# A windowed-attention and Mish feed-forward kernel: TensorE's instructions fixed in the program's order from chunk 2 on, an attention pair's values joined with the next pair's scores, and priorities for a step's functions

## The chip, the cores and the metric

The kernel runs on one core of one Trainium2 chip. The metric is the time in microseconds (us) of one execution on the device, from its start to its end. Three executions of the kernel before gave 993.93, 995.66 and 997.05 us, so the median is 995.66 us. A profiled execution is a fourth one; its own time is used where its trace is read.

A core has five engines that run side by side. TensorE (PE in the profile) multiplies matrices into PSUM; its weight loads are shown apart as PEld. VectorE (DVE), ScalarE (ACT) and GpSimd (POOL) do elementwise work. SyncE (SP) here only issues DMA transfers. The program gives each engine its own list of instructions; one that waits for another engine holds up those behind it on its list.

## The reference, cut to what matters

```python
def _attn_ref(q, k, v):                      # q, k, v: (8, 8, 576, 64)
    scores = scale * np.matmul(q, k.transpose(0, 1, 3, 2))
    rel = pos[:, None] - pos[None, :]
    mask = (rel >= 0) & (rel < 64)           # a window of 64 keys
    scores = np.where(mask, scores, -1e9)
    scores = scores - np.max(scores, axis=-1, keepdims=True)
    attn = np.exp(scores)
    attn = attn / (np.sum(attn, axis=-1, keepdims=True) + 1e-09)
    return np.matmul(attn, v)

def _moe_ref(x, w_in, w_out):                # x: (4608, 512), d_ff = 2048
    h = x @ w_in
    sp = np.where(h > 20.0, h, np.log1p(np.exp(np.minimum(h, 20.0))))
    g = h * np.tanh(sp)
    return g @ w_out
```

The output of the attention, with the heads laid side by side, is the `x` of the feed-forward part. All is float32.

## The kernel before, in words

**Chunks, steps and pairs.** The 4608 tokens are cut into 12 chunks of 384. The feed-forward part of a chunk is 16 *steps*, one for each 128 of the 2048 hidden columns. A step has a first product (`ffn_in`, 12 matmuls of 128x384 into one PSUM tile `h_ps`, line 195), a chain of functions, and a second product (`ffn_out`, 9 matmuls of 128x512 into the three sums `acc`, line 230). Twelve and nine, because every float32 factor is split into a high and a low part (`xh`, `xl`; `wi_h`, `wi_l`; `gh`, `gl`; `wo_h`, `wo_l`) and three of the four products are taken. The functions of a step run on DVE (line 202), ACT (203, 208, 209, 210), DVE (212) and POOL (216, 217; ACT line 214 in chunk 0). `h_ps` has two buffers, and line 212 is its last reader. The second product of a step is put into the program two steps behind its first one (`LAG = 2`).

The attention of a chunk is done in four *pairs* of heads. A pair has `scores` (24 small matmuls into two `s_ps`, line 128, then the masked minimum on DVE, line 138, six exponentials on ACT, line 141, and the normalisation on DVE, lines 149 to 151), `transpose`, and `values` (24 small matmuls into `o_ps`, line 184, then `xh` on ACT, line 186, and `xl` on DVE, line 187). For chunks 1 and 2 the transpose is six TensorE transposes (line 171) with a copy out of PSUM on ACT and one on DVE (line 172). For chunks 3 and up it is one DVE transpose of 32x32 blocks (line 160) and twelve DMA transfers from `tr` to `pT`, issued by SP (line 165).

**The weights** are loaded and split during chunk 0's steps (`load_w`): DVE lines 252 to 256 and 258, ACT lines 251 and 257, POOL lines 252 and 258.

**What sets the order.** The first 8 steps belong to chunk 0; then steps of chunks 0 and 1 alternate; from chunk 2 on one chunk follows the other. Each step has two *slots*. The attention of a chunk is a list of events with a slot each: scores at `begin + p*step`, transpose at `+0.6*step`, values at `+lag*step`. In the loop a step's `ffn_in` is traced, then the events due by slot 2n, then the `ffn_out` of two steps back, then the events due by slot 2n+1:

```python
    for n, (c, f) in enumerate(steps):
        ...
        pend.append((c, f, ffn_in(c, atts[c].x, f, c == NCHUNK - 1)))
        run(2 * n)
        if len(pend) > LAG:
            flush()
        run(2 * n + 1)
```

For chunks 3 and up the events begin with the first step of the chunk before and are 6 slots (3 steps) apart, values one spacing after the scores. So the values of pair p and the scores of pair p+1 are due in the same slot; the key puts the values first.

This trace order isn't the order on the engines. The kernel is built with `schedule_with_timeline_sim=True`: a planner goes through a simulated time and gives each engine the next instruction that is ready by then, and among ready ones the one that was traced first. What is ready depends on the planner's cost of each instruction and on free buffers (`h_ps` 2; the tag `at` for `s_ps`, `t_ps`, `o_ps` 3; `t` 4, shared by the functions and the splitting of weights; `pr` 2, shared by `pr` and `tr`). So a group of 12, 9 or 24 matmuls may come out in pieces with other work between them. The order that results is fixed in the program; the chip waits where an instruction isn't ready.

Of the kernel before, what the change touches and what calls it, by code (L numbers as in the profile page):

```python
# [2 lines left out]

# [15 lines left out]
BLK = 64  # L19
TINY = float(np.array(0x38000000, np.uint32).view(np.float32))  # L20
BIG = float(np.array(0x47EFFFFF, np.uint32).view(np.float32))
WP = 512


@with_exitstack
def tile_window_attn_mish_ffn(
# [60 lines left out]
    pTs = itertools.cycle(pTs)  # L87

    sums = itertools.cycle([f"acc{t}" for t in range(NTT)])
# [25 lines left out]
    def att_scores(c, p, tiles):  # L118
        q_t, k_t = tiles
        s_ps = [bank(c, p, "s_ps").rearrange("p (m k) -> p m k", k=P) for _ in range(2)]  # L120
        pr = ap_.tile([P, HM, P], F32, name="pr", bufs=2)
        mx = ap_.tile([P, HM], F32, name="mx", bufs=3)
        sm = ap_.tile([P, HM], F32, name="sm", bufs=3)
        for m in range(NM):
            for par, h in ((0, 0), (1, 1), (1, 0), (0, 1)):
                n = 2 * m + par
                rows = slice(h * BLK, (h + 1) * BLK)
                nc.tensor.matmul(s_ps[h][par * BLK:(par + 1) * BLK, m, :],  # L128
                                 q_t[rows, n * BLK:(n + 1) * BLK], k_t[rows, n * BLK:n * BLK + P],
                                 start=True, stop=True)  # L130
        for h in range(2):
            js = slice(h * NM, (h + 1) * NM)
            for m in range(NM):
                first = [(c * NB + 2 * m + par) % blocks_per_seq == 0 for par in range(2)]
                mk = firsts[first.index(True)] if any(first) else mask
                j = h * NM + m

                nc.vector.tensor_tensor_reduce(  # L138
                    out=pr[:, j, :], in0=s_ps[h][:, m, :], in1=mk,
                    op0=ALU.add, op1=ALU.min, scale=-0.125, scalar=3.0e38, accum_out=mx[:, j:j + 1])  # L140
                nc.scalar.activation(pr[:, j, :], pr[:, j, :], AF.Exp, bias=mx[:, j:j + 1], scale=-1.0,  # L141
                                     accum_out=sm[:, j:j + 1])
            if c == 0:

                nc.vector.tensor_scalar(sm[:, js], sm[:, js], 1e-9, None, ALU.add)
                nc.vector.reciprocal(sm[:, js], sm[:, js])
                nc.vector.tensor_tensor(pr[:, js, :], pr[:, js, :], sm[:, js].unsqueeze(2).to_broadcast([P, NM, P]), ALU.mult)
        if c > 0:
            nc.vector.tensor_scalar(sm, sm, 1e-9, None, ALU.add)
            nc.vector.reciprocal(sm, sm)  # L150
            nc.vector.tensor_tensor(pr, pr, sm.unsqueeze(2).to_broadcast([P, HM, P]), ALU.mult)
        return pr

    def att_transpose(c, p, pr):
        pT = next(pTs)
        if c > 2:


            tr = ap_.tile([P, P // 32, HM, 32], F32, name="tr", tag="pr", bufs=2)
            nc.vector.transpose(tr.rearrange("p k j i -> p j k i"),  # L160
                                pr.rearrange("p j (k i) -> p j k i", i=32))
            for r in range(0, P, 32):
                for k in range(0, P, 32):
                    if 0 <= k - r % BLK <= BLK:
                        nc.sync.dma_start(pT[k:k + 32, r // 32, :, :], tr[r:r + 32, k // 32, :, :])
            return pT
        for h in range(2):
            t_ps = (bank(c, p, "t_ps") if c else ps_h.tile([P, CH], F32, name="t_ps", tag="h_ps")
                    ).rearrange("p (m k) -> p m k", k=P)
            for m in range(NM):  # L170
# [4 lines left out]
        return pT  # L175

    def att_values(c, p, v_t, pT, x):
        xh, xl = x
        o_ps = bank(c, p, "o_ps")
        for n in range(NB):  # L180
            m, par = n // 2, n % 2
            for h in range(2):
                rows = slice(h * BLK, (h + 1) * BLK)
                nc.tensor.matmul(o_ps[rows, n * BLK:(n + 1) * BLK], v_t[:, n, rows],  # L184
                                 pT[:, 2 * par:2 * par + 2, h * NM + m, :], start=True, stop=True)
        nc.scalar.copy(xh[:, p, :], o_ps)
        nc.vector.tensor_tensor(xl[:, p, :], o_ps, xh[:, p, :].bitcast(F32), ALU.subtract)

    def ffn_in(c, x, f, alone=False):
        xh, xl = x  # L190
# [1 line left out]
        n = 0  # L192
        for cc in range(NC_):
            for w, xx in ((wi_h, xh), (wi_h, xl), (wi_l, xh)):
                nc.tensor.matmul(h_ps, w[:, f, cc, :], xx[:, cc, :], start=n == 0, stop=n == 3 * NC_ - 1)  # L195
# [6 lines left out]
        nc.vector.tensor_scalar(t, h_ps, 20.0, None, ALU.min)  # L202
        nc.scalar.activation(t, t, AF.Exp)  # L203
        if alone:

            h = ap_.tile([P, CH], F32, name="h", tag="pr", bufs=2)
            nc.scalar.copy(h, h_ps)
        nc.scalar.activation(t, t, AF.Square, bias=one_b)  # L208
        nc.scalar.activation(t, t, AF.Ln, bias=half_b, scale=0.5)  # L209
        nc.scalar.activation(t, t, AF.Exp, scale=-1.0)  # L210

        nc.vector.scalar_tensor_tensor(t, t, -1.0, h, ALU.add, ALU.mult)  # L212
        if c == 0:
            nc.scalar.copy(gh, t)  # L214
        else:
            nc.gpsimd.tensor_scalar(gh, t, 1.0, 0.0, ALU.mult, ALU.add)  # L216
        nc.gpsimd.tensor_tensor(gl, t, gh.bitcast(F32), ALU.subtract)  # L217
        return gh, gl

    half_b = const.tile([P, 1], F32, name="half_b")  # L220
# [4 lines left out]
    def ffn_out(acc, gg, f):  # L225
        gh, gl = gg
        for t in range(NTT):
            ts_ = slice(t * P, (t + 1) * P)
            for i, (a, w) in enumerate(((gh, wo_h), (gh, wo_l), (gl, wo_h))):
                nc.tensor.matmul(acc[t], a[:, ts_], w[:, f, :],  # L230
                                 start=f == 0 and i == 0, stop=f == NF - 1 and i == 2)

    def ffn_store(c, acc):
        for t in range(NTT):
            o = mp.tile([P, DO], F32, name="o", bufs=3, tag="st")
            if t % 2 == 0:
                nc.scalar.mul(o, acc[t], -1.0)
            else:
                nc.vector.tensor_scalar(o, acc[t], -1.0, None, ALU.mult)
            nc.sync.dma_start(out[c * CH + t * P:c * CH + (t + 1) * P, :], o)  # L240

    def load_w(src, wh, wl, first):
# [25 lines left out]
    class Att:  # L268
# [11 lines left out]
                getattr(a, what)[p] = {"qk": load_qk, "v": load_v}[what](a.c, p)  # L280

        def scores(self, p):
            self.pr[p] = att_scores(self.c, p, self.qk[p])
            self.load(p + 2, "qk")

        def transpose(self, p):
# [2 lines left out]
        def values(self, p):  # L289
            if self.x is None:  # L290
                self.x = tuple(xp.tile([P, NC_, CH], F32R, name=f"x{n}{self.c % 2}") for n in "hl")
            att_values(self.c, p, self.v[p], self.pT.pop(p), self.x)
            self.load(p + 2, "v")

        def plan(self, begin, step, lag=1):
# [65 lines left out]
    take_w(1)  # L361
    atts[1].plan(0, 2 * HEAD / (NPAIR + 1))
    atts[2].plan(third, (starts[2] - third) / (NPAIR + 1), 1.5)
    for c in range(3, NCHUNK):
        atts[c].plan(starts[c - 1], (2 * NF - 2) / (NPAIR + 1))
    events.sort(key=lambda e: e[:2])
    for n, (c, f) in enumerate(steps):
        if f == 0:

            while any(fn.__self__ is atts[c] for _, _, fn, _ in events):  # L370
                run(events[0][0])
        pend.append((c, f, ffn_in(c, atts[c].x, f, c == NCHUNK - 1)))
        run(2 * n)
        if len(pend) > LAG:
            flush()
        run(2 * n + 1)
        if c == 0:
            take_w(2)
    while pend:
        flush()  # L380


# [33 lines left out]
```

## Time and profile before

| | |
|---|---|
| median of three executions | 995.66 us (993.93 to 997.05) |
| the profiled execution | 995.3 us, of which 993.5 us from its first to its last instruction |
| mean granted TensorE clock | 0.972 |
| PE busy | 946.5 us (95%) |
| DVE, ACT, POOL busy | 491.8, 631.4, 328.8 us |
| chain that ended last | PE 87%, DVE 6%, DMA 2%, ACT 2% |

The chain of waits is followed back from the last instruction; its shares say which engine's work set the end. A matmul's duration in the trace is longer than the time to the next start, because matmuls overlap. So this document takes the cost of a group of matmuls from starts: from its first start to the first start of what follows.

In the rows of the timeline the columns are start and duration in us, engine, line, operation, `out<-in`, tile sizes, how many were merged into the row, and in brackets the idle time before it and what ended that. In the rows of waits they are who waited, for whom, the total in us, how many times, the longest. In the rows of windows they are the window, its length, busy time and instructions of each engine, the granted clock, the share of DMA and GB/s.

### The profile page before, as it was taken

Reading aid. Unit: us, or ns where it says so; the run is one execution under the profiler, and the core shown is the slowest. Engines: PE = TensorE matmul, PEld = TensorE weight load, DVE = VectorE, ACT = ScalarE, POOL = GpSimd, SP = SyncE. Lnnn points to the kernel's source line nnn. Section 1 sums busy time; section 2 is a strip of 40 time slices with the busy share of each in tenths; the row PEclk is TensorE's granted clock in tenths of the full one; section 3 lists DMA queues with packets and bytes.
Section 4 is the critical chain, followed back from the end, with each engine's and each line's share of the span. In section 5 each row is a group of like instructions: output and inputs, shape, how many; then the busy total and the mean of one; then the engine's idle time right before and its main releaser. Section 6 shows DMA issues by size and latency. Waiting matters only on the chain.

```text
span 993.5 us, 18088 instructions
## 1 busy us (share of the span) xinstructions
PE 946.5 (95%) x6408; PEld 821.4 (83%) x6408; DVE 491.8 (50%) x1352; ACT 631.4 (64%) x1525; POOL 328.8 (33%) x419
## 2 busy tenths in 40 slices
PE   4696699998999999999999999999999999999998
PEld 3585599886888888888888888888888888888996
DVE  6799874444444454444454453453443543543222
ACT  5667676664666666665665666666665665666664
POOL 2243463321333333323333323323333333333333
PEclk8787899997999999999999999999999999999999
DMA  7565420123221221331221221221231221310000
GB/s 240 188 194 161 143 85 1 49 68 111 66 69 54 89 69 42 88 83 42 88 83 43 89 81 45 86 83 46 84 80 47 85 74 43 97 39 13 32 1 32
DMA packets 82649, 77.34 MB, mean 78 GB/s; under 512 B 10368, under 2 KB 73856, under 8 KB 82560
## 3 DMA queue, kind: packets, MB, share of 16 engines
q1 hardware_dynamic: 82560, 76.19, 25.5%
q8 instruction: 51, 0.84, 0.4%
q14 instruction: 38, 0.31, 0.1%
HBM read 56.10 MB, written 9.44 MB: 66 GB/s over the span
## 4 chain that ended last, share of the span: by engine, by line
PE 87%; DVE 6%; DMA 2%; ACT 2%; issue 1%; SPq 0%; ACTq 0%; POOL 0%; DVEq 0%; POOLq 0%
PE h_ps L195 40%; PE acc L230 38%; PE s_ps L128 4%; PE o_ps L184 4%; DMA st<-w_out 2%; DVE wa L256 1%; DVE wa L255 1%; DMA st<-w_in 1%; ACT pr L141 1%; PE t_ps L171 1%; DVE wa L252 0%; DVE wi_l L258 0%; DVE wa L254 0%; DVE t L212 0%; ACT wa L251 0%
## 5 line engine op out<-in xcount | busy, mean ns | idle before, releaser
L195 PE MATMUL h_ps<-xh,wi_h 128*128 128x384 f32 x768 | 267.8, 349 | 13.6 <-DVE t L212 12.3
L216 POOL TENSOR_SCALAR gh<-t 128x384 fp32r<-128x384 f32 x176 | 90.7, 515 | 550.1 <-DVE t L212 504.0
L195 PE MATMUL h_ps<-xh,wi_l 128*128 128x384 f32 x768 | 263.7, 343 | 0.0
L195 PE MATMUL h_ps<-xl,wi_h 128*128 128x384 f32 x768 | 263.3, 343 | 0.0
L203 ACT ACTIVATE t<-t 128x384 f32<-128x384 f32 x192 | 100.5, 524 | 237.2 <-DVE t L202 237.2
L230 PE MATMUL acc<-wo_l,gh 128*128 128x512 f32 x576 | 227.0, 394 | 0.0
L230 PE MATMUL acc<-wo_h,gh 128*128 128x512 f32 x576 | 226.4, 393 | 0.5 <-POOL gh L216 0.5
L212 DVE SCALAR_TENSOR_TENSOR t<-t,h_ps 128x384 f32<-128x384 f32 x176 | 96.9, 550 | 250.3 <-ACT t L210 249.9
L217 POOL TENSOR_TENSOR gl<-t,gh 128x384 fp32r<-128x384 f32 x192 | 197.2, 1027 | 32.8 <-ACT gh L214 18.2
L230 PE MATMUL acc<-wo_h,gl 128*128 128x512 f32 x576 | 206.8, 394 | 0.0
L195 PEld LDWEIGHTS h_ps<-xh,wi_h 128*128 128x128 f32 x768 | 147.0, 192 | 28.5 <-DVE t L212 14.6
L195 PEld LDWEIGHTS h_ps<-xl,wi_h 128*128 128x128 f32 x768 | 147.4, 192 | 8.1 <-issue 1.9
L195 PEld LDWEIGHTS h_ps<-xh,wi_l 128*128 128x128 f32 x768 | 147.5, 192 | 1.1 <-issue 0.2
L202 DVE TENSOR_SCALAR t<-h_ps 128x384 f32<-128x384 f32 x192 | 106.6, 556 | 63.2 <-PE h_ps L195 55.8
L141 ACT ACTIVATE pr<-pr,mx 128x128 f32<-128x128 f32 x288 | 111.8, 390 | 38.0 <-DVE mx L138 38.0
L230 PEld LDWEIGHTS acc<-wo_h,gl 128*128 128x128 f32 x576 | 107.4, 188 | 23.7 <-issue 1.5
L230 PEld LDWEIGHTS acc<-wo_h,gh 128*128 128x128 f32 x576 | 109.1, 189 | 17.6 <-POOL gh L216 0.9
L230 PEld LDWEIGHTS acc<-wo_l,gh 128*128 128x128 f32 x576 | 108.9, 189 | 16.6
L209 ACT ACTIVATE t<-t,half_b 128x384 f32<-128x384 f32 x192 | 118.2, 616 | 5.4
L208 ACT ACTIVATE t<-t,one_b 128x384 f32<-128x384 f32 x192 | 118.1, 616 | 5.1
L210 ACT ACTIVATE t<-t 128x384 f32<-128x384 f32 x192 | 100.4, 524 | 5.6
L138 DVE CUSTOM_DVE_ANT_0 pr<-s_ps,mask 128x128 f32<-128x128 f32 x288 | 65.3, 286 | 60.7 <-PE s_ps L128 60.7
(49 smaller groups left out, 693.3 us busy)
## 6 DMA issues: line engine op xcount, KB each, us to landing
v_t<-vN SPq DMA_DIRECT2D x48, 384.0 KB, 3.6
k_t<-kT SPq DMA_DIRECT2D x47, 224.0 KB, 3.0
pT<-tr SPq DMA_DIRECT2D x432, 24.0 KB, 1.8
out<-o SPq DMA_DIRECT2D x36, 256.0 KB, 2.3
q_t<-qT SPq DMA_DIRECT2D x47, 192.0 KB, 2.5
st<-w_in SPq DMA_DIRECT2D x16, 512.0 KB, 4.4
st<-w_out SPq DMA_DIRECT2D x16, 512.0 KB, 3.4
q_t<-qT SPq DMA_DIRECT2D x3, 64.0 KB, 2.1
```

The costliest lines, as they stand in the source:

```text
L138: nc.vector.tensor_tensor_reduce(out=pr[:, j, :], in0=s_ps[h][:, m, :], in1=mk, op0=ALU.add, op1=ALU.min, scale=-0.125, scalar=3.0e38, acc ...
L141: nc.scalar.activation(pr[:, j, :], pr[:, j, :], AF.Exp, bias=mx[:, j:j + 1], scale=-1.0, accum_out=sm[:, j:j + 1])
L195: nc.tensor.matmul(h_ps, w[:, f, cc, :], xx[:, cc, :], start=n == 0, stop=n == 3 * NC_ - 1)
L202: nc.vector.tensor_scalar(t, h_ps, 20.0, None, ALU.min)
L203: nc.scalar.activation(t, t, AF.Exp)
L208: nc.scalar.activation(t, t, AF.Square, bias=one_b)
L209: nc.scalar.activation(t, t, AF.Ln, bias=half_b, scale=0.5)
L210: nc.scalar.activation(t, t, AF.Exp, scale=-1.0)
L212: nc.vector.scalar_tensor_tensor(t, t, -1.0, h, ALU.add, ALU.mult)
L216: nc.gpsimd.tensor_scalar(gh, t, 1.0, 0.0, ALU.mult, ALU.add)
L217: nc.gpsimd.tensor_tensor(gl, t, gh.bitcast(F32), ALU.subtract)
L230: nc.tensor.matmul(acc[t], a[:, ts_], w[:, f, :], start=f == 0 and i == 0, stop=f == NF - 1 and i == 2)
```

## The change

Four things are done.

1. All matmuls of the two feed-forward products, the scores and the values go through `pe()`, which notes them in a list. From the first `ffn_in` of chunk 2 on, each of these groups is traced inside `in_order()`: every TensorE instruction of the group gets an edge to the last matmul traced before the group. It is an edge of order only, with no wait on the chip. Within a group the planner is still free, and TensorE's transposes aren't in the list.
2. The first matmul of a pair's values gets a dependency on all twelve transfers of its `pT`, so that the group starts when all have landed.
3. The events of chunks 3 and up are spread anew. Those of chunk 3 begin 7 slots into chunk 2 and are 4.75 slots apart; from there each chunk's first scores are due 6 slots before the chunk that precedes it begins, with 8 slots (4 steps) between pairs. So there is one group of values and scores every fourth step, and a chunk's last values are due 6 slots before its own first step. Chunk 3's transposes are done on TensorE (the condition is `c > 3`), not by DMA.
4. The functions of a step, the copies `xh` and `xl` and the copies of the finished sums are traced under `high_priority(offset=400)`: the planner treats them as if they had been traced 400 instructions earlier. This holds for all chunks.

```diff
+SYNC = mybir.DependencyInfo(mybir.DependencyClass.Sync, mybir.DependencyReason.DATA)
+SOON = 400
...
+    order = []
+    ordered = []
+
+    def pe(*args, **kw):
+        order.append(nc.tensor.matmul(*args, **kw).ins)
+
+    def in_order():
+        return tc.issue_after(order[-1]) if ordered else nullcontext()
...
     def att_transpose(c, p, pr):
         pT = next(pTs)
-        if c > 2:
+        if c > 3:
+            moved = []
...
-                        nc.sync.dma_start(pT[k:k + 32, r // 32, :, :], tr[r:r + 32, k // 32, :, :])
-            return pT
+                        moved.append(nc.sync.dma_start(pT[k:k + 32, r // 32, :, :], tr[r:r + 32, k // 32, :, :]))
+            return pT, moved
...
     def att_values(c, p, v_t, pT, x):
+        pT, moved = pT
...
-                nc.tensor.matmul(o_ps[rows, n * BLK:(n + 1) * BLK], v_t[:, n, rows],
-                                 pT[:, 2 * par:2 * par + 2, h * NM + m, :], start=True, stop=True)
-        nc.scalar.copy(xh[:, p, :], o_ps)
-        nc.vector.tensor_tensor(xl[:, p, :], o_ps, xh[:, p, :].bitcast(F32), ALU.subtract)
+                pe(o_ps[rows, n * BLK:(n + 1) * BLK], v_t[:, n, rows],
+                   pT[:, 2 * par:2 * par + 2, h * NM + m, :], start=True, stop=True)
+                for d in moved:
+                    tc.add_manual_dep(order[-1], d.ins.name, SYNC, reason="values in one piece")
+                moved = []
+        with tc.high_priority(offset=SOON):
+            nc.scalar.copy(xh[:, p, :], o_ps)
+            nc.vector.tensor_tensor(xl[:, p, :], o_ps, xh[:, p, :].bitcast(F32), ALU.subtract)
...
     def ffn_in(c, x, f, alone=False):
...
-        nc.vector.tensor_scalar(t, h_ps, 20.0, None, ALU.min)
...
+        with tc.high_priority(offset=SOON):
+            nc.vector.tensor_scalar(t, h_ps, 20.0, None, ALU.min)
...
     def ffn_store(c, acc):
...
+            with tc.high_priority(offset=SOON):
+                if t % 2 == 0:
+                    nc.scalar.mul(o, acc[t], -1.0)
+                else:
+                    nc.vector.tensor_scalar(o, acc[t], -1.0, None, ALU.mult)
...
         def scores(self, p):
-            self.pr[p] = att_scores(self.c, p, self.qk[p])
+            with in_order():
+                self.pr[p] = att_scores(self.c, p, self.qk[p])
             self.load(p + 2, "qk")
...
-            att_values(self.c, p, self.v[p], self.pT.pop(p), self.x)
+            with in_order():
+                att_values(self.c, p, self.v[p], self.pT.pop(p), self.x)
             self.load(p + 2, "v")
...
+    ahead = 6
+    begin = starts[2] + ahead + 1
     for c in range(3, NCHUNK):
-        atts[c].plan(starts[c - 1], (2 * NF - 2) / (NPAIR + 1))
+        atts[c].plan(begin, (starts[c] - ahead - begin) / NPAIR)
+        begin = starts[c] - ahead
...
-        pend.append((c, f, ffn_in(c, atts[c].x, f, c == NCHUNK - 1)))
+        if c == 2 and f == 0:
+            ordered.append(True)
+        with in_order():
+            pend.append((c, f, ffn_in(c, atts[c].x, f, c == NCHUNK - 1)))
         run(2 * n)
         if len(pend) > LAG:
-            flush()
+            with in_order():
+                flush()
         run(2 * n + 1)
```

More of the change, by code (lines that the diff above doesn't have):

```diff
@@ L1 @@
 import itertools
-from contextlib import ExitStack
+from contextlib import ExitStack, nullcontext
 import numpy as np
@@ L127, in att_scores @@
                 rows = slice(h * BLK, (h + 1) * BLK)
-                nc.tensor.matmul(s_ps[h][par * BLK:(par + 1) * BLK, m, :],
-                                 q_t[rows, n * BLK:(n + 1) * BLK], k_t[rows, n * BLK:n * BLK + P],
+                pe(s_ps[h][par * BLK:(par + 1) * BLK, m, :],
+                   q_t[rows, n * BLK:(n + 1) * BLK], k_t[rows, n * BLK:n * BLK + P],
                                  start=True, stop=True)
@@ L174, in att_transpose @@
                 t_ps.rearrange("p m (r i) -> p m r i", i=32))
-        return pT
+        return pT, []
     def att_values(c, p, v_t, pT, x):
+        pT, moved = pT
         xh, xl = x
@@ L194, in ffn_in @@
             for w, xx in ((wi_h, xh), (wi_h, xl), (wi_l, xh)):
-                nc.tensor.matmul(h_ps, w[:, f, cc, :], xx[:, cc, :], start=n == 0, stop=n == 3 * NC_ - 1)
+                pe(h_ps, w[:, f, cc, :], xx[:, cc, :], start=n == 0, stop=n == 3 * NC_ - 1)
                 n += 1
@@ L201, in ffn_in @@
         h = h_ps
[L202 to L217, printed above, removed]
+        with tc.high_priority(offset=SOON):
+            nc.vector.tensor_scalar(t, h_ps, 20.0, None, ALU.min)
+            nc.scalar.activation(t, t, AF.Exp)
+            if alone:
+                h = ap_.tile([P, CH], F32, name="h", tag="pr", bufs=2)
+                nc.scalar.copy(h, h_ps)
+            nc.scalar.activation(t, t, AF.Square, bias=one_b)
+            nc.scalar.activation(t, t, AF.Ln, bias=half_b, scale=0.5)
+            nc.scalar.activation(t, t, AF.Exp, scale=-1.0)
+            nc.vector.scalar_tensor_tensor(t, t, -1.0, h, ALU.add, ALU.mult)
+            if c == 0:
+                nc.scalar.copy(gh, t)
+            else:
+                nc.gpsimd.tensor_scalar(gh, t, 1.0, 0.0, ALU.mult, ALU.add)
+            nc.gpsimd.tensor_tensor(gl, t, gh.bitcast(F32), ALU.subtract)
         return gh, gl
@@ L229, in ffn_out @@
             for i, (a, w) in enumerate(((gh, wo_h), (gh, wo_l), (gl, wo_h))):
-                nc.tensor.matmul(acc[t], a[:, ts_], w[:, f, :],
+                pe(acc[t], a[:, ts_], w[:, f, :],
                                  start=f == 0 and i == 0, stop=f == NF - 1 and i == 2)
@@ L235, in ffn_store @@
             o = mp.tile([P, DO], F32, name="o", bufs=3, tag="st")
[L236 to L239, printed above, removed]
+            with tc.high_priority(offset=SOON):
+                if t % 2 == 0:
+                    nc.scalar.mul(o, acc[t], -1.0)
+                else:
+                    nc.vector.tensor_scalar(o, acc[t], -1.0, None, ALU.mult)
             nc.sync.dma_start(out[c * CH + t * P:c * CH + (t + 1) * P, :], o)
@@ L379, in tile_window_attn_mish_ffn @@
     while pend:
-        flush()
+        with in_order():
+            flush()
 def kernel(**inputs):
```

## The prediction

> **What bounds the kernel now.** I read the page first: busy time, the slices, the chain.
>
> ```profile
> span 993.5 us, 18088 instructions
> PE 946.5 (95%) x6408; PEld 821.4 (83%) x6408; DVE 491.8 (50%) x1352; ACT 631.4 (64%) x1525; POOL 328.8 (33%) x419
> PE   4696699998999999999999999999999999999998
> PEclk8787899997999999999999999999999999999999
> PE 87%; DVE 6%; DMA 2%; ACT 2%; issue 1%; SPq 0%; ACTq 0%; POOL 0%; DVEq 0%; POOLq 0%
> ```
>
> A slice is 24.8 us. PE has gaps in the first five slices and once more near 240 us; from the eleventh slice to the end it is never below 90%, at full clock. So three stages have to be costed apart, and the windows cut there say the same:
>
> ```profile
> 35.00:131.00 96.00, 76.90 (x483) 65.61 (x482) 84.57 (x179) 66.25 (x157) 39.01 (x33) 0.83 0.51 161
> 222.00:254.00 32.00, 27.39 (x224) 22.84 (x223) 13.73 (x46) 16.48 (x47) 6.07 (x8) 0.84 0.28 88
> 254.00:918.00 664.00, 664.00 (x4606) 577.03 (x4605) 301.67 (x884) 422.03 (x1031) 213.53 (x280) 1.00 0.23 68
> ```
>
> The first is the head, where DVE is busy 84.57 of 96 us with splitting weights. The second is the start of chunk 2. In the third, 664 us long, PE has no idle time at all: only less PE work, or less lost between PE's instructions, can shorten it.
>
> **What a step costs on PE.** Starts in the timeline of PE, in a stretch without attention:
>
> ```profile
> 620.07 0.34 PE L195 MATMUL h_ps<-xh,wi_h 128*128 128x384 f32 x1
> ...
> 622.15 0.39 PE L230 MATMUL acc<-wo_h,gh 128*128 128x512 f32 x1
> ...
> 624.20 0.34 PE L195 MATMUL h_ps<-xh,wi_h 128*128 128x384 f32 x1
> ```
>
> The 12 first products take 2.08 us (0.173 each), the 9 second products 2.05 (0.228 each), a step 4.13.
>
> **What a pair costs on PE now.** The first four of a pair's values come back at the same place of every chunk, in these rows eight chunks apart:
>
> ```profile
> 268.00 0.34 PE L184 MATMUL o_ps<-pT,v_t 128*64 128x64 f32 x4
> 268.27 0.89 PE L128 MATMUL s_ps<-k_t,q_t 64*64 64x128 f32 x24
> ...
> 284.35 0.34 PE L184 MATMUL o_ps<-pT,v_t 128*64 128x64 f32 x4
> 284.62 0.89 PE L128 MATMUL s_ps<-k_t,q_t 64*64 64x128 f32 x24
> 285.43 0.45 PE L195 MATMUL h_ps<-xl,wi_h 128*128 128x384 f32 x1
> ...
> 286.21 0.80 PE L184 MATMUL o_ps<-pT,v_t 128*64 128x64 f32 x20
> 286.94 0.50 PE L230 MATMUL acc<-wo_l,gh 128*128 128x512 f32 x1
> ...
> 874.75 0.34 PE L184 MATMUL o_ps<-pT,v_t 128*64 128x64 f32 x4
> ```
>
> A chunk lasts (874.75 - 268.00)/8 = 75.84 us. Sixteen steps are 16 x 4.13 = 66.1, so four pairs take 9.76, a pair 2.44. The rows show why it is that much: the values come as a piece of 4 (0.27) and one of 20 (0.73), with feed-forward matmuls between, in the middle of a group.
>
> **What a joined run costs.** Near 201 us half a pair's scores and a whole pair of values stand together:
>
> ```profile
> 201.28 0.40 PE L230 MATMUL acc<-wo_h,gh 128*128 128x512 f32 x1
> 201.60 0.87 PE L128 MATMUL s_ps<-k_t,q_t 64*64 64x128 f32 x12
> 202.41 0.92 PE L184 MATMUL o_ps<-pT,v_t 128*64 128x64 f32 x24
> 203.26 0.50 PE L230 MATMUL acc<-wo_l,gh 128*128 128x512 f32 x1
> 203.59 0.40 PE L230 MATMUL acc<-wo_h,gl 128*128 128x512 f32 x1
> ```
>
> Going in costs 0.32 - 0.23 = 0.09 us, going out 0.33 - 0.23 = 0.10, and from scores to values nothing beyond the 0.81. 24 values in one piece are 0.85; 24 scores in one piece are 0.81 (284.62 to 285.43). So a run of values and scores is 0.09 + 0.85 + 0.81 + 0.10 = 1.85; I take 1.89, since the first matmul after a run is late by up to 0.13 in other places. That is 0.55 below 2.44: 0.14 for the values in one piece, the rest for one entry and exit where there were two or three.
>
> **The change, part by part, against the profiled execution's own 995.3 us.**
>
> *Runs.* Attention of chunks 3 to 11 is 36 pairs, now 36 x 2.44 = 87.8 us. After: chunk 3's first scores alone (0.81 + 0.23 = 1.04), 35 joined runs (66.2), the last values alone (1.08): 68.3. That is -19.5. The bounds: if the planner still cuts values and scores apart, 0; if a run costs 1.85, -21.
>
> *Chunk 3's transposes on TensorE.* A group of six:
>
> ```profile
> 209.35 0.82 PE L171 MATMUL t_ps<-ident,pr 128*128 128x128 f32 x6
> 210.09 0.87 PE L128 MATMUL s_ps<-k_t,q_t 64*64 64x128 f32 x12
> ```
>
> 0.74 us, and 0.1 to 0.2 for its own entry and exit: four groups, +3.4. The 48 transfers they replace were not on PE's path. ACT and DVE take one copy each per pair; both have room in this stage (422 and 302 of 664 us).
>
> *The wait for all twelve transfers.* Here the order that the change imposes can cost something: behind the first matmul of the values stand the next scores and all feed-forward work, and nothing can be taken in its place. So I work out when `pT` is there. Of the pair whose scores end at 269.08:
>
> ```profile
> 269.60 0.28 DVE L138 CUSTOM_DVE_ANT_0 pr<-s_ps,mask 128x128 f32<-128x128 f32 x1
> ...
> 274.46 0.98 DVE L160 STREAM_TRANSPOSE tr<-pr 128x768 f32<-128x768 f32 x1
> 275.47 7.48 SPq L165 DMA_DIRECT2D pT<-tr  x12
> ```
>
> `tr` is done 6.4 us after the scores, SP issues the twelve transfers in 7.5 us, and the values started at 284.35, 8.9 after the first issue. They need all twelve, so that is an upper bound for the last landing: 6.4 + 8.9 = 15.3. After the change a run follows a first product, and the functions go first. On ACT they are
>
> ```profile
> L203 ACT ACTIVATE t<-t 128x384 f32<-128x384 f32 x192 | 100.5, 524 | 237.2 <-DVE t L202 237.2
> L141 ACT ACTIVATE pr<-pr,mx 128x128 f32<-128x128 f32 x288 | 111.8, 390 | 38.0 <-DVE mx L138 38.0
> L209 ACT ACTIVATE t<-t,half_b 128x384 f32<-128x384 f32 x192 | 118.2, 616 | 5.4
> L208 ACT ACTIVATE t<-t,one_b 128x384 f32<-128x384 f32 x192 | 118.1, 616 | 5.1
> L210 ACT ACTIVATE t<-t 128x384 f32<-128x384 f32 x192 | 100.4, 524 | 5.6
> ```
>
> 0.52 + 0.62 + 0.62 + 0.52, some 2.35 us with their gaps. Counted from the end of that first product: functions on ACT 0.7 to 3.1, `xh` to 3.5, six exponentials of 0.39 to 5.8. The scores end at 1.75, the next first product ends at 6.0, and its functions reach ACT at 6.7: the exponentials just fit between. The normalisation, one function (line 202, 0.5) and the transpose bring `tr` to 8.7, 7.0 after the scores. The last landing comes 15.9 after the scores. The values come four steps and an exit and entry later, 4 x 4.13 + 0.2 = 16.7. There is 0.8 us to spare, so 0 for most runs. Once in each chunk the stores of the finished sums share SP's queue, and the copies of the sums come before line 160:
>
> ```profile
> 320.95 1.60 SPq L240 DMA_DIRECT2D out<-o  x3
> ```
>
> 1.6 us, less the 0.8 to spare: a stall of about 0.7. Chunks 4 to 11 have one such run each: +5.6. The bounds are 0 (the stores go after the transfers) and 1.5 for every one of the 32 runs (below, the slower rival).
>
> *Functions first, in the head.* The list of waits, and its two largest places:
>
> ```profile
> PE h_ps L195 <- DVE t L212: 12.3, 4, 6.3
> ...
> 100.55 0.45 PE L195 MATMUL h_ps<-xh,wi_h 128*128 128x384 f32 x1 [2.35 <-DVE t L212]
> 123.82 0.69 PE L195 MATMUL h_ps<-xh,wi_h 128*128 128x384 f32 x1 [6.31 <-DVE t L212]
> ```
>
> PE stood still because line 212 hadn't freed `h_ps`, while DVE was splitting weights; a wait of PE for a weight tile isn't in the list. With functions first these 8.7 us can go. Against it: DVE is busy 88% of that stage, so every function that goes ahead delays a weight, and PE may then wait for weights instead. The bounds are -8.7 and, if the same waits come back doubled for weights, +8.7. I take -5, nearer to the gain because the weights show no wait now.
>
> *The start of chunk 2.* Now:
>
> ```profile
> 236.73 0.62 PE L195 MATMUL h_ps<-xh,wi_h 128*128 128x384 f32 x2 [1.27 <-ACT xh L186]
> 242.17 0.69 PE L195 MATMUL h_ps<-xh,wi_h 128*128 128x384 f32 x1 [3.34 <-DVE t L212]
> ```
>
> Before the last values of chunk 2 (at 234.55) the planner had put chunk 1's last two second products and parts of chunk 2's first two steps, then waited 3.34 us for their functions. In order, these fillers (2 x 2.05 and 16 x 0.173, together 6.9 us) come after the values: up to 6.9 more idle time before them, while afterwards a second product stands between any two first ones, so the waits of 4.6 and most of the half-clock loss (0.16 of 32 us, 5.1) vanish. Chunk 3's first scores also leave this place, and with them six exponentials ahead of `xh`. Bounds -9.7 and +6.9; I take 0. The clock is what could tip this. In that window it was granted at 0.84, with first products 0.32 apart until 247.8. The Trainium skill ("TensorE: Matmul & The Clock Gate", section on HAM oscillation) says that a PE idle for more than about 3.4 us drops to half its clock and then needs some 3.4 us of work to come back, which speaks against a strict order with a long wait at its start. By that rule one such drop would add an estimated 1.7 us and the sum would be 981.5; the trace agrees that the clock falls about such a wait.
>
> *No cost.* The edges within PE's queue are no instructions. The last chunk has no attention, its 16 steps run without stalls today, and its end (PE waits 0.5 us for the last `gh`) stays.
>
> Sum: 995.3 - 19.5 + 3.4 (together -16.1) + 5.6 - 5 + 0 = 979.8, so **980 us**. The profiled execution is 0.4 under the median; that is less than the median's own spread.
>
> **The rivals.**
>
> *Slower: `pT` comes late in every run.* If the six exponentials don't fit between two steps' functions, they are split by one chain of 2.35 us on ACT. The last landing is then 15.9 + 2.35 = 18.25 after the scores against 16.7, and PE, with nothing to put in its place, stalls 1.5 us in each of the 32 runs: +48, and 995.3 - 16.1 - 5 + 48 = 1022. It undoes the gain from about 0.65 us of stall per run, that is 1.5 us more on the chain. For it: the space for the exponentials has only 0.9 us to spare. Against it: the same chain took 15.3 without the second product that now stands behind the scores.
>
> *Faster still.* The head's waits all go, stores don't disturb, chunk 2's start gains 3: 995.3 - 16.1 - 8.7 - 3 = 967.
>
> *Only the runs.* The head gains nothing and chunk 2's start costs its 6.9: 995.3 - 16.1 + 5.6 + 6.9 = 992. For it: DVE's 88%.
>
> *The order doesn't make one piece.* Edges bind groups, not matmuls, and scores need two of the three `at` buffers at the moment the values take the third. If they are held back, a run falls apart again, the 19.5 is gone, and the transposes remain: 995.3 + 3.4 = 999.
>
> **How the numbers follow.** 980 (974 to 987) 0.45; faster still 0.20; only the runs 0.15; pieces remain 0.06; late `pT` 0.14. A difference of 0.3%, 3 us, is what a measurement of this kernel can tell from none. Faster: 0.45 + 0.20 + 0.12 of the third + 0.02 of small lateness = 0.79; the same 0.08; slower 0.13. The range for 8 in 10 goes from 964, a little under the second case, to 1000, which takes in the third, the fourth and a mild lateness.
>
> **What would show it.** Right: in PE's timeline every fourth step a row of 24 values followed by one of 24 scores, chunks 73.6 to 74.4 us apart where 75.84 stood, six transposes four times in chunk 2 only. Stalls: waits of PE at line 184 for `pT`, about 0.7 us, eight of them; 32 of them of over 1 us mean the slower rival. Head: waits for line 212 gone or shorter before 131 us; waits for weight tiles in their place would prove that term wrong. Start of chunk 2: no wait for line 212, a longer one before line 184 or 195. What makes the prediction wrong is above all the 0.8 us to spare.

## The result and the profile after

The changed kernel takes 979.69 us (median of four executions, 978.54 to 981.9), the kernel before beside it 995.26 (four executions). The ratio is 0.9845, 95% interval 0.9821 to 0.987. The forecast was 980. The profiled execution took 981.9 us, the one of before 995.3, so the traces show 13.4 of the 15.6 us between the medians; the changed kernel's profiled execution is the slowest of its four. Of all the executions told of below one stands apart, of 2323 us, in the ninth experiment; no ratio contains it.

The page of the changed kernel, the lines that answer to those shown of before:

```profile
span 980.1 us, 18009 instructions
PE 932.2 (95%) x6432; PEld 825.7 (84%) x6432; DVE 490.5 (50%) x1352; ACT 624.7 (64%) x1529; POOL 327.2 (33%) x419
...
PE   4797779998999999999999999999999999999997
...
PEclk9787889998999999999999999999999999999999
...
PE 85%; DVE 6%; DMA 3%; ACT 3%; issue 2%; SPq 1%; POOL 0%; ACTq 0%; DVEq 0%; POOLq 0%
```

The picture is the same, with gaps in the first slices and one near 240 us, but PE's busy time is 14.3 us less. Its instructions are 24 more, chunk 3's transposes. So what shrank is the time that they take one after another, not their number.

Where it went is read from the first first-product of a step in the timeline of PE, before and after. Chunk 1's last step, then the first of chunks 3 and 11. Before:

```profile
217.01 0.34 PE L195 MATMUL h_ps<-xh,wi_h 128*128 128x384 f32 x1
312.45 0.44 PE L195 MATMUL h_ps<-xh,wi_h 128*128 128x384 f32 x1
917.78 0.34 PE L195 MATMUL h_ps<-xh,wi_h 128*128 128x384 f32 x1
```

After:

```profile
220.96 0.34 PE L96 MATMUL h_ps<-xh,wi_h 128*128 128x384 f32 x1
314.98 0.34 PE L96 MATMUL h_ps<-xh,wi_h 128*128 128x384 f32 x1
904.15 0.34 PE L96 MATMUL h_ps<-xh,wi_h 128*128 128x384 f32 x1
```

| stage | before, us | after, us | difference | forecast |
|---|---|---|---|---|
| to chunk 1's last step | 217.01 | 220.96 | +3.95 | -5 |
| from there to chunk 3 | 95.44 | 94.02 | -1.4 | +1.2 |
| chunks 3 to 10 | 605.33 | 589.17 | -16.2 | -11.7 |
| chunk 11 to the end of the span | 75.7 | 75.95 | +0.2 | 0 |
| sum | 993.5 | 980.1 | -13.4 | -15.5 |

The forecast column splits the forecast's terms among the stages: four pairs' runs at -0.55 and the transposes' +3.4 make +1.2 in the second, the rest of the runs' -19.5 (-17.3) and the eight stalls (+5.6) are the third's -11.7. The total came close by luck. The head was lost and not won, 9 us worse than forecast; against it, the stalls at the stores (5.6 us) didn't come, and the start of chunk 2 went 2.6 us better. The runs and the transposes came out as worked out.

A run, and the values of the next run (18.41 us later) and of the one four runs after that, in the changed kernel's timeline:

```profile
321.02 0.34 PE L96 MATMUL h_ps<-xh,wi_l 128*128 128x384 f32 x1
321.29 0.92 PE L96 MATMUL o_ps<-pT,v_t 128*64 128x64 f32 x24
322.14 0.89 PE L96 MATMUL s_ps<-k_t,q_t 64*64 64x128 f32 x24
322.95 0.50 PE L96 MATMUL acc<-wo_h,gh 128*128 128x512 f32 x1
323.29 0.39 PE L96 MATMUL acc<-wo_l,gh 128*128 128x512 f32 x1
...
339.70 0.92 PE L96 MATMUL o_ps<-pT,v_t 128*64 128x64 f32 x24
...
413.35 0.92 PE L96 MATMUL o_ps<-pT,v_t 128*64 128x64 f32 x24
```

24 values take 0.85, 24 scores 0.81, entry and exit 0.10 and 0.11: 1.87 where the forecast had 1.89. From 339.70 to 413.35 is a chunk: 73.65 us, forecast 73.64.

And the list of PE's waits:

```profile
PE t_ps L184 <- DVE pr L163: 11.9, 3, 7.0
PE h_ps L96 <- DVE t L233: 11.3, 2, 7.5
...
PE o_ps L96 <- DMA pT<-tr: 0.7, 1, 0.7
```

One wait for the transfers, of 0.7 us, in the whole execution. The functions' wait (line 233 is before's 212) has not gone: 11.3 us where the list had 12.3.

### The profile page after: what moved, and what is told of

Same layout as the page of the kernel before. It is cut to its first block, busy times and chain, and to the rows that moved or that the text cites. A ratio compares the mean times of both kernels' runs of the same rounds, so it can differ in the third digit from the quotient of the medians.

```text
span 980.1 us, 18009 instructions
## 1 busy us (share of the span) xinstructions
PE 932.2 (95%) x6432; PEld 825.7 (84%) x6432; DVE 490.5 (50%) x1352; ACT 624.7 (64%) x1529; POOL 327.2 (33%) x419
## 4 chain that ended last, share of the span: by engine, by line
PE 85%; DVE 6%; DMA 3%; ACT 3%; issue 2%; SPq 1%; POOL 0%; ACTq 0%; DVEq 0%; POOLq 0%
PE h_ps L96 39%; PE acc L96 38%; PE s_ps L96 4%; PE o_ps L96 4%; DMA st<-w_in 1%; DVE wa L278 1%; DVE wa L277 1%; DMA st<-w_out 1%; SPq L178 1%; ACT pr L153 1%; DVE wa L276 1%; PE t_ps L184 1%; DVE t L223 1%; DVE t L233 0%; ACT wa L273 0%
## 5 line engine op out<-in xcount | busy, mean ns | idle before, releaser
L96 PE MATMUL h_ps<-xh,wi_h 128*128 128x384 f32 x768 | 263.8, 344 | 11.4 <-DVE t L233 11.3
L96 PE MATMUL acc<-wo_h,gh 128*128 128x512 f32 x576 | 229.2, 398 | 0.9 <-POOL gh L237 0.9
L238 POOL TENSOR_TENSOR gl<-t,gh 128x384 fp32r<-128x384 f32 x192 | 197.6, 1029 | 30.8 <-ACT gh L235 16.2
L96 PE MATMUL acc<-wo_h,gl 128*128 128x512 f32 x576 | 204.6, 392 | 0.0
L150 DVE CUSTOM_DVE_ANT_0 pr<-s_ps,mask 128x128 f32<-128x128 f32 x288 | 64.8, 285 | 15.9 <-PE s_ps L96 15.8
```

What stands on the lines that cost most here:

```text
L96: order.append(nc.tensor.matmul(*args, **kw).ins)
L150: nc.vector.tensor_tensor_reduce(out=pr[:, j, :], in0=s_ps[h][:, m, :], in1=mk, op0=ALU.add, op1=ALU.min, scale=-0.125, scalar=3.0e38, acc ...
```

## The experiments

Twelve kernels were run, most with several executions beside the kernel before on the same chip. Where one execution is given, there was one.

**1. No priorities.**

```diff
-with tc.high_priority(offset=SOON):
+with nullcontext():
```

> The changed kernel with part 4 (the priorities) taken out everywhere. In the changed kernel the head lost 4 us against before (first product of step (1,2) at 138.44 us, before 134.26) where I had forecast a gain of 5. Theory P: the priorities do that, by changing the planner's order among functions and weight splitting. Then the head comes back to before's (134.3), and the time is about 4 us below the changed kernel, 975 to 977, if the priorities do nothing for the later stages; if they keep the exponentials and functions in step there, runs stall and it is above 980. Theory H: the head moved for another reason (chunk 2's order reaching back); then 138.4 stays and the time is 979 to 981.

975.93 us, ratio 0.9818 (0.9795 to 0.9841). Step (1,2) is back at 134.38, chunk 1's last step at 216.93, as in the kernel before; runs and chunks as in the changed kernel (73.65 us from chunk 4 to 5). Theory P holds: the priorities cost the head time, and nothing later needs them. How much they cost is read from the first place at which the orders of the two kernels part. It is on DVE: with the priorities a function goes ahead of an attention pair's softmax, without them it does not. First the changed kernel, then this one:

```profile
76.02 0.55 DVE L223 TENSOR_SCALAR t<-h_ps 128x384 f32<-128x384 f32 x1
```

```profile
75.14 0.28 DVE L150 CUSTOM_DVE_ANT_0 pr<-s_ps,mask 128x128 f32<-128x128 f32 x1
```

From there to chunk 1's last step it is 144.94 us with the priorities and 141.79 without. The other traces say the same: 144.7 to 145.0 in the four kernels with the priorities in the head and shared buffers (the change, experiments 3, 4 and 9), 141.5 to 141.9 in the seven without (before, experiments 1, 2, 7, 8, 11 and 12). So the priorities cost 3.1 us. The rest of the 4 arose ahead of that place, where the order is the same with and without them; in the eleven traces it is reached anywhere between 73.0 and 77.9 us.

**2. Priorities only from chunk 2 on.**

```diff
+    def soon(c):
+        return tc.high_priority(offset=SOON) if c >= 2 else nullcontext()
-with tc.high_priority(offset=SOON):
+with soon(c):
```

> The changed kernel with the priorities only for chunks 2 and up. Theory P: head as before, later stages as in the changed kernel: 979.7 - 4 = 976 (0.9805 of before), first product of (1,2) at 134.3 us, chunks of 73.65 us. Theory H: 980, (1,2) at 138.4.

976.29 us, ratio 0.9818 (0.9805 to 0.9831), (1,2) at 134.62. Equal to the first experiment, and its trace has the same instructions in the same order on every engine. So the priorities do harm in the head, and from chunk 2 on they change nothing in this plan.

**3. No order.**

```diff
-        return tc.issue_after(order[-1]) if ordered else nullcontext()
+        return nullcontext()
```

> The changed kernel without the order edges on TensorE (part 1), everything else kept: the new spread of events, one wait for all transfers, priorities. If the order is what makes one piece of a pair, values and scores fall apart again and a chunk lasts over 75 us (pair 2.3 to 2.44): about 979.7 + 8 x 1.7 = 993, less some 3 to 5 at the start of chunk 2, where the planner may again put fillers ahead. If the wait for all transfers and the new spread already make the pieces whole, chunks stay at 73.65 us and the time at 978 to 982.

1017.76 us, ratio 1.023 (1.0213 to 1.0247): slower than the kernel before, and by far more than either expectation, so both were wrong. The pieces are whole (24 values and 24 scores together at 323.15, 343.28 and so on). What is lost is lost at the starts of chunks; the eighth experiment shows where.

**4. Seven slots between pairs.**

```diff
-        atts[c].plan(begin, (starts[c] - ahead - begin) / NPAIR)
+        atts[c].plan(begin, (starts[c] - ahead - begin) / NPAIR if c == 3 else 7)
```

> The changed kernel with 7 slots between pairs instead of 8 from chunk 4 on (values 3.5 steps after the scores). My theory: the transfers land about 16.0 us after the scores end (7.0 to tr, 7.5 of issuing, 1.6 to land), and the values now come 3.5 x 4.13 + 0.2 = 14.7 after them, so PE waits about 1.4 us at each of 32 values, plus what the functions of the first product that now follows the scores directly add: 45 us or more, time 1025 or above, with a list of waits that has the values on the transfers 32 times. Rival: there is far more to spare than 0.8 us, and it stays at 980.

1009.91 us (one execution; before 994.44), 30 above the changed kernel. Its waits and one pair:

```profile
PE o_ps L96 <- DMA pT<-tr: 24.5, 19, 2.3
```

```profile
768.59 0.89 PE L96 MATMUL s_ps<-k_t,q_t 64*64 64x128 f32 x24
769.41 0.50 PE L96 MATMUL acc<-wo_h,gh 128*128 128x512 f32 x1
...
785.44 0.92 PE L96 MATMUL o_ps<-pT,v_t 128*64 128x64 f32 x24 [1.28 <-DMA pT<-tr]
```

```profile
776.61 7.48 SPq L178 DMA_DIRECT2D pT<-tr  x12
```

The scores end at 769.41 and SP begins its issues 7.20 us later; the values start when the last transfer has landed, at 785.44: 16.03 us, the theory's 16.0. Over the 19 waits the values start 15.2 to 17.05 us after the scores, with 16.04 in the middle, and a wait is 1.3 us in the mean. There are fewer than 32 of them: where the chain on ACT and DVE is shorter, the landing just fits. The scores that end at 354.95, for instance, are followed by a first product, the issues begin 5.5 us after them, and the values at 369.63 don't wait. So the mechanism holds, and the expected 45 was too much by those runs. Half a step less room costs 30 us. Some 27 of them are waits before values, counting a few that the list puts down to other releasers. The edit does one thing more: with 7 slots a chunk's last values come 9 us ahead of the next chunk's first scores and no longer share a run with them, which costs a further entry and exit in each chunk.

**5 and 6. Two buffers for `t`, two for the weights' `wa`,** where four were shared; without priorities and with them.

```diff
-        t = mp.tile([P, CH], F32, name="t", tag="t", bufs=4)
+        t = mp.tile([P, CH], F32, name="t", tag="t", bufs=2)
-        a = mp.tile([P, WP], U32, name="wa", tag="t", bufs=4)
+        a = mp.tile([P, WP], U32, name="wa", tag="wa", bufs=2)
```

> The kernel without priorities, with the four buffers shared by the functions' t and the weights' wa split into two for each. Theory T: in the head the functions come late because no t buffer is free, so that they can't start whatever the planner prefers; then with two buffers of their own the waits of PE for line 233 (9.9 us in two places without priorities) shrink below 4 us and the head ends 3 to 8 us sooner: 968 to 973. Theory W: the head is bound by the splitting of weights on DVE itself; then less room for wa delays weights and the head ends at the same time or up to 6 us later: 976 to 982.

> The changed kernel (with priorities) with the same split of buffers. Theory T: now the priorities find a free buffer and can do what I had forecast; the head is no later than in the kernel without priorities and the same split, both 968 to 973. Theory W: functions put ahead still delay weights, and this kernel is again some 4 us slower than its fellow without priorities.

963.27 us without priorities (ratio 0.9678, 0.9658 to 0.9699), 963.21 with them (0.9679, 0.9659 to 0.9699). Theory T holds, and by more than it expected. In the window that the prediction showed of the head, without priorities first with shared buffers, then with the split:

```profile
35.00:131.00 96.00, 76.24 (x477) 64.87 (x478) 83.87 (x178) 66.44 (x158) 38.69 (x33) 0.81 0.50 160
```

```profile
35.00:131.00 96.00, 83.50 (x561) 71.14 (x561) 90.78 (x190) 74.04 (x173) 39.37 (x39) 0.94 0.51 161
```

DVE is busy 90.78 of 96 us where it was 83.87, PE's clock 0.94 where it was 0.81. The longest wait of a first product for line 233 falls from 6.1 to 1.4 us, and chunk 1's last step starts at 204.23 where 216.93 stood. Priorities no longer harm, because they no longer change the plan: the traces of the two kernels have the same instructions in the same order on every engine. Four buffers that anyone may take let the splitting of weights hold them while finished first products wait for one; that the split keeps two for the functions and that it holds the weights to two at a time are the same edit here, and which of the two does it was not told apart.

**7. No joint wait** (the dependency on the twelve transfers), no priorities.

```diff
-                for d in moved:
-                    tc.add_manual_dep(order[-1], d.ins.name, SYNC, reason="values in one piece")
```

> The kernel without priorities, and without part 2, the dependency of the first values on all twelve transfers; order and spread stay. Values of the first column block need six of the transfers, the next two the other six, so nothing is won by starting early and the order keeps the feed-forward matmuls out. I expect the same as with it, 975 to 977, pieces of 24 or of 2 and 22 with no other work between. Rival: the dependency is what makes one piece; then values come in 4 and 20 with scores or feed-forward matmuls between, +0.14 to 0.5 us in each of 32 runs, 980 to 992.

977.75 us, ratio 0.982 (0.9799 to 0.9841), rows of 24 values and 24 scores as before, and the same order of instructions on every engine as in the first experiment. With the order the joint wait isn't needed.

**8. Only spread and joint wait:** no order, no priorities.

```diff
-        return tc.issue_after(order[-1]) if ordered else nullcontext()
+        return nullcontext()
...
-        with tc.high_priority(offset=SOON):
+        with nullcontext():
```

> Only parts 2 and 3: the new spread with chunk 3's transposes on TensorE and one wait for all transfers; no order, no priorities. The kernel without order but with priorities took 1017.8 us: at the start of each chunk both h_ps buffers were held by first products that waited for the last pair, and PE waited 2.6 to 5.9 us for line 233. If the missing order alone does that, this kernel is as slow, 1010 to 1020. If the priorities drove the planner to it, chunks start without a wait and the time is 975 to 985.

1016.12 us, ratio 1.0206 (1.0177 to 1.0235). It is the missing order that does it, with priorities (the third experiment) or without. Around the start of chunk 5 in its timeline:

```profile
458.51 0.34 PE L96 MATMUL h_ps<-xh,wi_h 128*128 128x384 f32 x1
...
462.12 0.34 PE L96 MATMUL h_ps<-xh,wi_h 128*128 128x384 f32 x1
...
463.77 0.92 PE L96 MATMUL o_ps<-pT,v_t 128*64 128x64 f32 x24
...
473.33 0.69 PE L96 MATMUL h_ps<-xh,wi_h 128*128 128x384 f32 x1 [4.50 <-DVE t L233]
...
473.82 0.52 PE L96 MATMUL h_ps<-xl,wi_h 128*128 128x384 f32 x1
```

The planner takes nine matmuls of the chunk's first step (458.51) and nine of its second (462.12) before the last pair's values (463.77). Both `h_ps` are then held, the second products that could have filled in are used up, and PE waits 4.50 us for the functions of both steps at once; after that its clock is half (0.49 us to the next start). That is what happened at the start of chunk 2 before the change, now at the starts of chunks 5 to 10, with waits of 2.63 to 4.50 us. The plan itself holds the values back, and not the chip: over the 32 pairs they start 16.7 to 20.3 us after their scores, although the trace has the last transfers landed 14.2 to 16.2 us after them, and in the changed kernel they start after 16.75 (17.51 once). So each pair slips, until a chunk's last values fall behind the next chunk's first step. The old spread, whose last values were due 8 slots ahead of the chunk and not 6, had escaped it.

**9. Only the priorities,** in the kernel before, on the same instructions.

```diff
+        with tc.high_priority(offset=400):
             nc.vector.tensor_scalar(t, h_ps, 20.0, None, ALU.min)
...
```

> The kernel before with part 4 alone, the priorities, for all chunks. If they cost the head its 4 us wherever they stand and do nothing later: 995 + 4 = 999. If in the old order they keep the functions on time at the starts of chunks, under 995.

1000.72 us, ratio 1.0064 (1.0044 to 1.0085). Chunk 1's last step starts at 220.03, 3 us late; that is not won back: chunk 11 starts at 922.96 where 917.78 stood. Of these 5.2 us, 2.2 were lost behind chunk 1. So in the old order the priorities cost something later too: a chunk takes 75.99 us where it took 75.85.

**10. Only the split of the buffers,** in the kernel before.

```diff
-        t = mp.tile([P, CH], F32, name="t", tag="t", bufs=4)
+        t = mp.tile([P, CH], F32, name="t", tag="t", bufs=2)
...
-        a = mp.tile([P, WP], U32, name="wa", tag="t", bufs=4)
+        a = mp.tile([P, WP], U32, name="wa", tag="wa", bufs=2)
```

> The kernel before with only the four shared buffers split into two for t and two for wa, nothing of the change. The same split took 12.7 us off the kernel without priorities, all of it ahead of chunk 1's last steps. If that is independent of the order from chunk 2 on: 995 - 12.7 = 982, with step (1,15) 12 to 14 us sooner than before's 217.0. If the planner loses it again at chunk 2's start: 985 to 995.

981.46 us, ratio 0.9869 (0.9849 to 0.989); (1,15) at 203.45, 13.6 us sooner. Two buffer counts are worth nearly as much as the whole change, and add to it without its priorities: 0.9869 x 0.9818 = 0.969, measured 0.9678.

**11. Order and joint wait with the old spread** of 6 slots from chunk 4 on, no priorities.

```diff
-        atts[c].plan(begin, (starts[c] - ahead - begin) / NPAIR)
+        if c == 3:
+            atts[c].plan(begin, (starts[c] - ahead - begin) / NPAIR)
+        else:
+            atts[c].plan(starts[c - 1], (2 * NF - 2) / (NPAIR + 1))
```

> Order and one wait as in the kernel without priorities, but from chunk 4 on the old spread of 6 slots (3 steps) between a pair's scores and its values. The last transfer lands 16.0 us after the scores, the values come 3 x 4.13 + 0.2 = 12.6 after them: a wait of 3.4 us at each of 32 values, 976 + 109 = 1085, seen as waits on the transfers 32 times with about 3.4 us each. If the order itself were what saves the time, whatever the spread, it would stay below 995.

1090.61 us (one execution; before 993.6). Its waits:

```profile
PE o_ps L96 <- DMA pT<-tr: 78.4, 28, 5.5
```

28 waits of 2.8 us in the mean, not 32 of 3.4, and the total is still as expected, since after the longer of these waits PE runs at half its clock for a while (below). The order saves nothing by itself: without room for the transfers this kernel is 115 us slower than the first experiment's.

**12. Chunk 3's transposes by DMA** as before, no priorities.

```diff
-        if c > 3:
+        if c > 2:
```

> The kernel without priorities, with chunk 3's transposes by DMA as before (c > 2). Its pairs are 4.75 slots apart, so the values come about 2.4 x 4.13 = 9.8 us after the scores and would wait for transfers that land after 16.0: 6.2 us at each of 4 values, +25, less the 3.4 of the transposes on TensorE that go: 976 + 21 = 997. If the 3.4 were just lost: 972.

999.17 us (one execution; before 993.6), 23 above the first experiment, where the theory had 21:

```profile
265.95 1.55 PE L96 MATMUL o_ps<-pT,v_t 128*64 128x64 f32 x24 [4.38 <-DMA pT<-tr]
283.13 1.55 PE L96 MATMUL o_ps<-pT,v_t 128*64 128x64 f32 x24 [3.62 <-DMA pT<-tr]
300.27 1.55 PE L96 MATMUL o_ps<-pT,v_t 128*64 128x64 f32 x24 [3.57 <-DMA pT<-tr]
317.75 1.54 PE L96 MATMUL o_ps<-pT,v_t 128*64 128x64 f32 x24 [4.46 <-DMA pT<-tr]
```

16 us of waits and half a clock after each. The waits are 4.0 us each and not the 6.2 expected; the half clock, which the theory didn't have, makes up for that. What TensorE's transposes cost is well spent.

| kernel | us | against before |
|---|---|---|
| the change | 979.69 | 0.9845 |
| without priorities | 975.93 | 0.9818 |
| without priorities, buffers split | 963.27 | 0.9678 |
| only the buffers split | 981.46 | 0.9869 |
| only the priorities | 1000.72 | 1.0064 |
| only spread and joint wait | 1016.12 | 1.0206 |
| order and joint wait, old spread | 1090.61 | one execution |

## Why the prediction was right, point by point

**Runs, -19.5.** Right, by its own step. A run measured 1.87 for 1.89 and a chunk 73.65 for 73.64. Which part makes one piece was left open there. On the new spread the order is enough (seventh experiment) and so is the joint wait (eighth). The new spread without either was not run, so it isn't shown that one of them is needed. (One reading of the page of before was off and bears on nothing: in its last slice PE stands at 8, below 90%.)

**Chunk 3's transposes, +3.4.** The sign is right and the reason is the forecast's (9.8 us are not enough for DMA), as the twelfth experiment shows. The size can be estimated from the changed kernel: chunk 2's second to sixteenth step take 74.1 us; less 15 x 4.13, four runs of 1.87 and 0.91 for the first scores alone, 3.7 us are left for the four groups, 0.5 of which are waits for `pT` at one of them.

**The landing, 0.8 us to spare.** Right. `tr` is done 6.5 to 7.15 us after the scores, mostly 6.9 (forecast 7.0), and in the fourth experiment, where the values wait for the last landing, they start 16.04 after the scores in the middle of 19 (forecast 15.9), against 16.7. The slower rival was close: with 3.5 steps in the place of 4 the kernel is slower than before (1009.91), with 3 far slower. In the changed kernel the room was missing once:

```profile
561.42 0.92 PE L96 MATMUL o_ps<-pT,v_t 128*64 128x64 f32 x24 [0.69 <-DMA pT<-tr]
```

There SP took 8.62 us for the twelve issues that take 7.5 for most pairs. The stores of that chunk had been issued 2 us before, so they are not the reason, which stays open.

**Eight stalls at the stores, +5.6.** Wrong: none; the one wait of 0.69 above is not the stores'. The step that failed is "the stores of the finished sums share SP's queue" at the time of the transfers. SP in the changed kernel, at that place of chunk 4's stretch:

```profile
326.13 2.03 SPq L262 DMA_DIRECT2D out<-o  x3
330.16 7.49 SPq L178 DMA_DIRECT2D pT<-tr  x12
```

The stores are out 2 us before `tr` is ready. With two steps of lag the last second product of a chunk follows the first product of the next chunk's second step, which is the very step of the run, so the sums are finished and stored while the softmax is still at work. The lower bound, 0, was given for the opposite case, stores that go after the transfers.

**The head, -5.** Wrong in sign: +3.95, of which 3.1 are due to the priorities (first experiment). The step said that PE stood still because line 212 came late "while DVE was splitting weights", and that functions put first would take that wait away. The wait was real, but priority is no cure for it: with shared buffers the wait stays (9.9 us in two places without priorities, 11.3 with them), with buffers of their own it is 5.2 us in seven places, none longer than 1.4, whether there are priorities or not. The bound of +8.7 held this outcome, for another reason than the one given there, which was that weights would be late. The changed kernel around its longest wait, the last matmuls of the first products of steps (0,9) and (1,0) on PE, then DVE:

```profile
117.53 0.34 PE L96 MATMUL h_ps<-xh,wi_l 128*128 128x384 f32 x1
...
120.13 0.34 PE L96 MATMUL h_ps<-xh,wi_l 128*128 128x384 f32 x1
```

```profile
118.01 0.54 DVE L206 TENSOR_TENSOR xl<-o_ps,xh 128x384 fp32r<-128x384 f32 x1
...
119.42 0.41 DVE L276 TENSOR_SCALAR wa<-wa 128x512 uint32<-128x512 uint32 x1
119.86 0.69 DVE L277 SCALAR_TENSOR_TENSOR wa<-st,wa 128x512 uint32<-128x512 uint32 x1
120.59 0.69 DVE L278 SCALAR_TENSOR_TENSOR wa<-st,wa 128x512 uint32<-128x512 uint32 x1
121.20 1.01 DVE L223 TENSOR_SCALAR t<-h_ps 128x384 f32<-128x384 f32 x2
```

Step (1,0) had to wait for `xl` of its last pair. Line 223, which has the priority and needs a free `t`, comes for both steps at 121.20, 3.3 us after (0,9) is ready and behind the weights. That a free `t` is what it lacked is inferred from the fifth and sixth experiment; the trace doesn't show buffers. The priorities' 3.1 us arise between the steps (0,7) and (1,2), after functions have gone ahead of a softmax; through which instruction, was not settled.

**The start of chunk 2, 0.** Within its bounds. The second stage, forecast +1.2, measured -1.4, so this term was about -2.6, and half of that is a matter of chance: after the same wait the clock stayed at half for 6.8 us in the changed kernel (granted 0.50 from 231.6 to 238.3), for 3.4 in the fourth experiment, whose order up to there is the same (0.50 to 235.0, 1.00 behind it), and chunk 2 took 79.76 us in the one and 78.28 in the other. Before the last values PE now waits 2.76 us for the softmax, as feared, and runs the first product behind them at half clock for 3.1 us; but the waits of 1.27 and 3.34 us behind them are gone, as foreseen.

```profile
231.58 1.51 PE L184 MATMUL t_ps<-ident,pr 128*128 128x128 f32 x6 [2.76 <-DVE pr L163]
...
235.22 0.69 PE L96 MATMUL h_ps<-xh,wi_h 128*128 128x384 f32 x1
...
238.83 0.39 PE L96 MATMUL acc<-wo_h,gh 128*128 128x512 f32 x1
```

**What the prediction didn't see.** It gave the gain to the runs alone and none to the order. The third and eighth experiments show that the new spread without the order loses 21 to 23 us against the kernel before: the order is what keeps PE from starting a chunk's first steps too early. The part of the change with the largest effect is, on the new spread, one whose effect in the changed kernel is nowhere visible.

## What to carry to other kernels

When a wait names a function that is late, ask what it had to have before it could start: here a buffer that other work held, so that splitting one pool of four into two and two was worth 13 us, while priorities in the planner cost 3 with the shared pool and changed nothing with the split one. A fixed order on the busiest engine pays if what it waits for lands with room to spare, and this can be worked out from three rows (end of the scores, end of the issue, start of the values) to within a few tenths of a us; half a step less room turned a gain of 16 us into a loss of 15. And a planner that fills a gap with the next stage's first work can use up the very work that would have hidden that stage's latency.

## What the runs showed of the hardware

The clock after a wait could be read from the 24 values that follow it. In experiments 11 and 12 they took 0.92 us at full clock and 1.55 at half. After waits of up to 1.9 us they always took 0.92, after waits of 3.57 us and more always 1.55, and for the eight waits between 2.85 and 3.23 anything from the one to the other:

```profile
453.81 1.16 PE L96 MATMUL o_ps<-pT,v_t 128*64 128x64 f32 x24 [3.09 <-DMA pT<-tr]
...
719.73 0.92 PE L96 MATMUL o_ps<-pT,v_t 128*64 128x64 f32 x24 [3.01 <-DMA pT<-tr]
720.58 1.56 PE L96 MATMUL s_ps<-k_t,q_t 64*64 64x128 f32 x24
...
806.67 1.55 PE L96 MATMUL o_ps<-pT,v_t 128*64 128x64 f32 x24 [2.93 <-DMA pT<-tr]
```

Values in 0.92 don't mean that no drop came: behind those at 719.73 the scores take 1.56 us for their usual 0.89.

Elsewhere shorter waits were enough. In the changed kernel the clock fell at the wait of 2.76 us at 231.58. In the kernel before it fell 0.6 us behind the end of the wait of 1.27 us that the prediction shows, and ahead of the one of 3.34:

```profile
237.33 0.54 PE L195 MATMUL h_ps<-xl,wi_h 128*128 128x384 f32 x1
237.66 0.52 PE L195 MATMUL h_ps<-xh,wi_l 128*128 128x384 f32 x1
```

First products are 0.32 us apart from there on, where they are 0.173 at full clock. Ahead of both waits stood the small matmuls of scores, values and transposes; whether that matters was not tested.

The Trainium skill ("TensorE: Matmul & The Clock Gate", section on HAM oscillation) puts the drop to half clock at an idle time of about 3.4 us. The traces agree with it only roughly: in experiments 11 and 12 the drop came every time from 3.57 us of listed wait on, but elsewhere it also came at 2.76, and in the kernel before behind 1.27. So the prediction's remark that the clock falls about a wait of that length holds for experiments 11 and 12, and not for the place that it was read from.
